# Merged first-layer matmuls in a Strassen-style MLP: products in a group of three and one of four per pair, preparation at earlier places

## The chip, the cores and the metric

The kernel runs on one core of a Trainium2 chip, in one launch. The metric is device time in microseconds (us) of an execution, as the median of three runs. The core has five engines that run side by side, each working through its own instructions in order: PE (TensorE, with the weight loads shown apart as PEld), DVE (VectorE), ACT (ScalarE), POOL (GpSimd) and SP (SyncE, which issues the DMAs here).

## What is computed

First an attention with random features (batch 8, 8 heads, 576 tokens, head size 64, 128 features), then a mixing of tokens through U and V, then an MLP over 8 * 576 = 4608 tokens with 512 inputs, 2048 hidden units and 512 outputs. The change touches the MLP:

```python
u = x + h.transpose(0, 2, 1)                    # x: attention output, h: token mixing
ch = np.maximum(u @ w_ch1, 0.0) @ w_ch2
return (u + ch).astype(np.float32)
```

Every float32 operand of a matmul is split into a high and a low part of a reduced format (fp32r), and a product is the sum of three passes: high weight with high data, high weight with low data, low weight with high data.

## The kernel before

**Stages.** Attention and token mixing run until about 380 us; then a whole pass of the MLP over the first 6 tiles of 128 tokens; from 443 to 1031 us seven **chunks** (c = 1 to 7) of 4 tiles (512 tokens); then a whole pass over the last 2 tiles (c = 8). The loop over chunks is at L1090. It is in the seven chunks that the change works, and in the last six of them that it changes the matmuls.

**A pair.** In a chunk the 16 blocks of hidden units are taken two at a time: eight **pairs** (p = 0 to 7). The first layer of a pair, a product of 2 x 2 blocks (inputs by hidden units by tokens), is made in Winograd's form with **seven products** (i = 0 to 6) in place of eight (`products`, L925). A product takes a data operand `self.ops[i]` (tiles `ux`, `uy`: sums of blocks of the transposed tokens, high and low, 2 halves of 128 inputs, 256 tokens) and a weight operand `w.ops[i]` (tile `wx`). It is six matmuls of 128x256: two halves by three passes. They accumulate in four PSUM banks X, Y, Z, W: products 0 and 3 in X, 1 and 4 in Y, 2 and 6 in Z, 5 in W. `after(i)` then takes a bank out: ACT copies (L938) and relus (L919), DVE sums (L774, in the helper `sums`) and the low part of the relu (L921). The results g of a pair are the data of the second layer.

**The order on PE.** The second layer of pair p is a generator of 24 matmuls of 128x512 (`second`, L987; 4 token tiles x 2 blocks x 3 passes, written to PSUM tiles `p_n` and `p_q`). `take(steps, 1)` places the next one of them into the stream. While the products of pair p+1 run, two or three second-layer matmuls of pair p stand between the six of each product and one more in `between(i)`. So a pair is 42 narrow and 24 wide matmuls.

**What else `between(i)` places (L1103).** Its steps stand on their engines in program order: fetching the weights of the next pair (`new.add()`: one DMA of 256 KB from `wx_dram` per product on SP, into a ring of 8 tiles, so that operand j of the next pair goes into the tile that operand j-1 of this pair leaves), stores of finished outputs (`stores`: a DVE sum L1008 and a DMA), and preparing the next chunk: `fetch` (L364: four DMAs on SP that bring 128 inputs of the next chunk's tokens into a tile `uraw`, of which there are two), `turn` (L858: a DVE transpose of a `uraw` tile into `uT`), `prepare` (L875: POOL sums of `uT` blocks) and `add` (L770 and L771: the split of an operand into high and low). Four `uraw` tiles are fetched per chunk, the third and fourth only behind the first and second turn, whose tiles they reuse. Turns stand in pairs 5 and 6 at i = 0 and 4, sums in pair 6, splits in pair 7.

Of the kernel before, what the change touches and what calls it, by code (L numbers as in the profile page):

```python
# [9 lines left out]
F32 = mybir.dt.float32  # L10
# [4 lines left out]
ALU = mybir.AluOpType  # L15
# [14 lines left out]
def performer_mlp_kernel(ctx: ExitStack, tc, q, k, v, omega, U, V, w1, w2, out):  # L30
# [27 lines left out]
    def f32(ap):  # L58
        return ap.bitcast(F32)
# [706 lines left out]
    keep = tc.keep_in_program_order  # L766

    def split(hl, x, rest=nc.gpsimd):

        keep(nc.scalar.copy(out=hl[:, 0], in_=x))  # L770
        keep(rest.tensor_tensor(out=hl[:, 1], in0=x, in1=f32(hl[:, 0]), op=SUBTRACT))  # L771

    def sums(out, a, b, op):
        keep(nc.vector.tensor_tensor(out=out, in0=a, in1=b, op=op))  # L774
# [64 lines left out]
    class Chunk:  # L839
# [37 lines left out]
        def prepare(self, part=(0, 1, 2)):  # L877

            for i in part:
                if i == 0:  # L880
                    self.sum(1, self.block(0, 1), self.block(0, 0), SUBTRACT)
                elif i == 1:
                    self.sum(2, self.block(1, 1), self.s[1], SUBTRACT)
                else:
# [12 lines left out]
        def whole1(self, w, between=lambda: None, every=lambda: None):  # L897
# [17 lines left out]
                between()  # L915
            return g

        def relu(self, g, ts, x, out=lambda: None):
            keep(nc.scalar.activation(out=g[:, 0, ts], in_=x, func=AF.Relu))  # L919
            out()  # L920
            keep(nc.vector.scalar_tensor_tensor(  # L921
                out=g[:, 1, ts], in0=x, scalar=0.0, in1=f32(g[:, 0, ts]), op0=ALU.max, op1=ALU.subtract
            ))

        def products(self, w, between, steps, out=lambda: None):  # L925

            bank = lambda n, b: ps.tile([P, HT], F32, name="p_s", tag=n, bufs=b)
# [6 lines left out]
            t1, t2 = slice(0, HT), slice(HT, TOK)  # L934

            def after(i):
                if i == 0:
                    keep(nc.scalar.copy(out=p1, in_=X))  # L938
                elif i == 1:
                    sums(u2, Y, p1, ADD)  # L940
                elif i == 3:
                    self.relu(g[0], t1, X)
                elif i == 4:
                    out()
                    sums(u3, Y, p1, ADD)
                    sums(c22, Z, u3, ADD)
                    self.relu(g[1], t2, c22, out)
                elif i == 5:
                    sums(c21, W, u3, ADD)
                    self.relu(g[1], t1, c21)  # L950
                elif i == 6:
                    sums(c12, Z, u2, ADD)
                    self.relu(g[0], t2, c12)

            for i, o in enumerate((X, Y, Z, X, Y, W, Z)):
                x, wt = self.ops[i], w.ops[i]
                for k in range(2):
                    for j, (l, r) in enumerate(passes((wt[:, 0, k], wt[:, 1, k]), (x[:, 0, k], x[:, 1, k]))):  # L960
                        tc.keep_in_program_order(nc.tensor.matmul(  # L961
                            o, l, r, start=(i in (0, 1, 2, 5) and k + j == 0), stop=(k == 1 and j == 2),
                            skip_group_check=True,
                        ))
                        if 3 * k + j in ((1, 3) if i % 2 else (0, 2, 3)):
                            take(steps, 1)
                after(i)
                between(i)
            return g

        def second(self, fs, gs, begin, end):
# [118 lines left out]
    for c in range(1, NCH - 1):  # L1090
        now, nxt = nxt, Chunk(c + 1)
        short = nxt.n < CT
        for p in range(NH):
            new = None
            if p + 1 < NH or not short:
                new = Weights(p + 1) if c == 1 and p + 1 < NH else Again((p + 1) % NH)
            if p < 2:
                nxt.fetch()
            if p == NH - 1:
                if not short:  # L1100
                    nxt.add()

            def between(i):  # L1103
                take(steps, 1)
                if p > 4 and i % 4 == 0 and nxt.turned < NC:
                    nxt.turn()
                    if nxt.turned < 3:
                        nxt.fetch()
                if p == 6 and not short and i in (2, 5, 6):
                    nxt.prepare([(2, 5, 6).index(i)])  # L1110
                if c == 1 and i < 2 and stores:
                    stores.pop(0)()
                if len(now.ops) < 7:
# [8 lines left out]
                for _ in range((0, 0, 0, 0, 0, 0, 2)[i] if c == 1 else 1):  # L1122
                    if stores:
                        stores.pop(0)()
                if p == NH - 1 and i < 6:
                    if not short:
                        nxt.add()
                    elif i in (0, 2):
                        nxt.short(nxt.uT[:, i : i + 2, :HT], nc.vector)
                    elif i in (1, 3):  # L1130
                        ws[i // 2] = Halves(i // 2)

            def out():
                if c == 1 and p == 0:
                    stores.pop(0)()

            g = now.products(pairs, between, steps, out)
# [47 lines left out]
```

## Time and profile before

| | us |
|---|---|
| runs before: median (lowest to highest of 3) | 1085.99 (1085.52 to 1086.03) |
| the profiled execution's own time | 1087.22 |
| its span in the trace | 1085.4 |
| PE busy, share of the span | 1074.5, 99% |
| DVE, ACT, POOL busy | 665.8, 502.3, 334.4 |
| from the first product of c = 1 to the last of c = 7 | 443.2 to 1030.8 |

The profile groups instructions by source line, engine and operation; "idle before" is time the engine stood still just ahead of them, with what ended it. A matmul's shown duration (280 ns for 128x256, some 393 ns for 128x512) is its whole way through the array, and matmuls overlap; what one costs is the distance from its start to the next one's start. The same holds in part on DVE.

### The profile page before, as it was taken

How to read it: one execution, taken by the hardware profiler on the slowest of the kernel's cores; microseconds unless marked ns; L12 is line 12 of the kernel's file. 1: busy time of each engine (PE TensorE's matmuls, PEld its weight loads, DVE VectorE, ACT ScalarE, POOL GpSimd, SP SyncE). 2: the span in 40 equal slices, each digit the busy share in tenths (PEclk: the TensorE clock that was granted, in tenths of full speed). 3: DMA queues.
4: the chain of work that ended last, by engine and by line, in shares of the span. 5: the costliest groups of instructions: out<-in, count | busy, mean ns of one | idle time of the engine just before them, and what ended most of it. 6: DMA issues, size and time to landing. Idle time of an engine off the chain costs nothing.

```text
span 1085.4 us, 20563 instructions
## 1 busy us (share of the span) xinstructions
PE 1074.5 (99%) x7119; PEld 974.3 (90%) x7119; DVE 665.8 (61%) x1460; ACT 502.3 (46%) x1417; POOL 334.4 (31%) x345
## 2 busy tenths in 40 slices
PE   9999999999999999999999999999999999999998
PEld 7899999999988888888888898988999888898987
DVE  4788998998977776655634734634643643643421
ACT  5799889998856664443321311311321321311232
POOL 3246547557445556565200100100100100100143
PEclk9999999999999999999999999999999999999999
DMA  8688887787224553565876876876885786785510
GB/s 138 129 149 146 169 177 150 172 169 130 79 86 141 146 149 94 201 216 195 254 212 173 251 218 156 257 232 156 234 256 166 221 254 163 216 253 158 181 59 20
DMA packets 344583, 187.93 MB, mean 173 GB/s; under 512 B 276128, under 2 KB 276128, under 8 KB 344480
## 3 DMA queue, kind: packets, MB, share of 16 engines
q1 hardware_dynamic: 342112, 186.32, 65.1%
q8 instruction: 57, 0.93, 0.4%
q10 hardware_dynamic: 2368, 0.30, 0.2%
q14 instruction: 46, 0.38, 0.1%
HBM read 152.99 MB, written 33.55 MB: 172 GB/s over the span
## 4 chain that ended last, share of the span: by engine, by line
PE 79%; DVE 4%; ACT 3%; POOL 2%; issue 2%; DMA 1%; SPq 0%; POOLq 0%; DVEq 0%; ACTq 0%
PE p_s L961 24%; PE p_n L987 17%; PE p_q L987 15%; PE p_p L910 6%; PE p_n L497 3%; PE p_kv L451 3%; PE p_p L539 2%; PE p_p L540 2%; PE p_p L541 2%; PE p_q L477 2%; PE py L334 2%; POOL mag L171 1%; DVE mag L149 1%; ACT e L554 1%; DMA kt<-in_k_dram 1%
## 5 line engine op out<-in xcount | busy, mean ns | idle before, releaser
L961 PE MATMUL p_s<-ux,wx 128*128 128x256 f32 x1728 | 363.8, 280 | 0.4 <-DVE far L774 0.3
L961 PEld LDWEIGHTS p_s<-ux,wx 128*128 128x128 f32 x1728 | 321.4, 188 | 31.6 <-DVE far L774 0.6
L987 PE MATMUL p_n<-w2h,g 128*128 128x512 f32 x576 | 219.1, 394 | 0.0
L987 PE MATMUL p_q<-w2h,g 128*128 128x512 f32 x512 | 195.4, 392 | 0.0
L554 ACT ACTIVATE e<-p_p,nm 128x128 f32<-128x128 f32 x576 | 166.3, 388 | 25.4 <-DVE nm L547 17.0
L961 PE MATMUL p_s<-uy,wx 128*128 128x256 f32 x624 | 132.6, 279 | 0.0
L420 POOL TENSOR_TENSOR xl<-xT,xh 128x384 fp32r<-128x384 f32 x95 | 94.5, 1014 | 116.7 <-ACT xh L416 90.8
L961 PEld LDWEIGHTS p_s<-uy,wx 128*128 128x128 f32 x624 | 117.0, 188 | 11.3 <-DMA wx<-wx_dram 0.3
L919 ACT ACTIVATE g<-far 128x256 fp32r<-128x256 f32 x112 | 46.8, 418 | 169.8 <-DVE far L774 169.8
L875 POOL TENSOR_TENSOR us<-uT 128x512 f32<-128x512 f32 x14 | 19.1, 1361 | 338.1 <-DVE uT L858 338.1
L987 PEld LDWEIGHTS p_n<-w2h,g 128*128 128x128 f32 x576 | 108.6, 188 | 9.3
L547 DVE TENSOR_REDUCE nm<-p_p 128x4 f32<-128x512 f32 x144 | 97.9, 680 | 25.5 <-PE p_p L541 16.9
L987 PE MATMUL p_n<-w2l,g 128*128 128x512 f32 x288 | 113.4, 394 | 0.0
L774 DVE TENSOR_TENSOR near<-p_s,near 128x256 f32<-128x256 f32 x168 | 70.3, 419 | 67.9 <-PE p_s L961 66.6
L771 POOL TENSOR_TENSOR wx<-w1f,wx 128x256 fp32r<-128x256 f32 x86 | 68.5, 811 | 135.1 <-ACT wx L770 133.5
L921 DVE SCALAR_TENSOR_TENSOR g<-p_s,g 128x256 fp32r<-128x256 f32 x56 | 23.7, 423 | 138.8 <-ACT g L919 138.7
L919 ACT ACTIVATE g<-p_s 128x256 fp32r<-128x256 f32 x56 | 21.5, 384 | 185.0 <-PE p_s L961 185.0
L987 PEld LDWEIGHTS p_q<-w2h,g 128*128 128x128 f32 x512 | 96.2, 188 | 9.9
L987 PE MATMUL p_q<-w2l,g 128*128 128x512 f32 x256 | 100.6, 393 | 0.0
L539 PE MATMUL p_p<-omh,xh 128*128 128x256 f32 x288 | 93.0, 323 | 1.7 <-ACT e L554 1.6
L910 PE MATMUL p_p<-ux,wx 128*128 128x512 f32 (+1 forms) x480 | 84.5, 326 | 0.2 <-DVE g L921 0.2
L921 DVE SCALAR_TENSOR_TENSOR g<-far,g 128x256 fp32r<-128x256 f32 x112 | 49.5, 442 | 53.9 <-ACT g L919 53.9
(133 smaller groups left out, 2055.8 us busy)
## 6 DMA issues: line engine op xcount, KB each, us to landing
wx<-wx_dram SPq DMA_DIRECT2D x336, 256.0 KB, 3.3
raw<-in_moe_w_ch_dram SPq DMA_DIRECT2D x32, 512.0 KB, 4.2
wx_dram<-wx SPq DMA_DIRECT2D x56, 256.0 KB, 2.0
u_dram<-x SPq DMA_DIRECT2D x36, 256.0 KB, 2.4
u<-u_dram SPq DMA_DIRECT2D x34, 256.0 KB, 4.6
out_dram<-u SPq DMA_DIRECT2D x34, 256.0 KB, 3.2
kt<-in_k_dram SPq DMA_DIRECT2D x120, 72.0 KB, 3.5
qt<-in_q_dram SPq DMA_DIRECT2D x120, 72.0 KB, 2.7
```

The costliest lines, as they stand in the source:

```text
L420: rest.tensor_tensor(out=self.xl[-1], in0=self.turned, in1=f32(self.xh[-1]), op=ALU.subtract)
L451: tc.keep_in_program_order(nc.tensor.matmul(o, e[:, h, :], w, start=(s == 0 and h == 0), stop=(s == NT - 1), skip_group_check=True))
L539: nc.tensor.matmul(o, part.xh[g][:, ts], oh, start=True, stop=False)
L547: nc.vector.tensor_reduce(out=self.nm[:, :n], in_=self.pp[:, :n], axis=AX.X, op=ALU.max, negate=True)
L554: nc.scalar.activation(out=self.e[:, j, :], in_=self.pp[:, j, :], func=AF.Exp, bias=self.nm[:, j : j + 1])
L771: keep(rest.tensor_tensor(out=hl[:, 1], in0=x, in1=f32(hl[:, 0]), op=SUBTRACT))
L774: keep(nc.vector.tensor_tensor(out=out, in0=a, in1=b, op=op))
L910: nc.tensor.matmul(ph, l, r, start=(cc + i == 0), stop=(cc == NC - 1 and i == 2))
L919: keep(nc.scalar.activation(out=g[:, 0, ts], in_=x, func=AF.Relu))
L921: keep(nc.vector.scalar_tensor_tensor(out=g[:, 1, ts], in0=x, scalar=0.0, in1=f32(g[:, 0, ts]), op0=ALU.max, op1=ALU.subtract))
L961: tc.keep_in_program_order(nc.tensor.matmul(o, l, r, start=(i in (0, 1, 2, 5) and k + j == 0), stop=(k == 1 and j == 2), skip_group_check= ...
L987: tc.keep_in_program_order(nc.tensor.matmul(po, l, r, start=(begin and n + i == 0), stop=(end and n == len(fs) - 1 and i == 2)))
```

## The change

For chunks 2 to 7, in all pairs but the last of a chunk (and in chunk 7 in that too), each product's passes are arranged otherwise. High and low parts of a data operand now lie side by side for each half, so one matmul of 128x512 with the high weight makes both "high with high" and "high with low" into the two halves of a full PSUM bank; a matmul of 128x256 with the low weight adds to the first half. A product is four matmuls in place of six. The two halves of a bank are added when it is taken out: more DVE sums, two more ACT copies, and the relu of product 3 reads the sum.

The matmuls are also regrouped. In pairs 0 to 5, products 0, 1, 2 form a group and 3, 4, 6, 5 another: all wide matmuls of the group, then all narrow ones, then twelve second-layer matmuls, then `after` and `between` for each of its products. In pair 6 (and 7 of chunk 7) there are four smaller groups. 43 pairs take the new form (five chunks of 7, one of 8); 13 keep the old one. The DVE part of a relu is put off behind the next product's sums (`pend`). For chunks from 2 on, turns move to pairs 2 and 3 at i = 2 and 6, sums to pairs 4 and 5 (the fourth sum gets a `uraw` tile of its own), the first split to pair 6, and stores to i = 1, 2, 5, 6.

```diff
-            split(self.slot(self.ops), x, nc.gpsimd if self.c == 1 and i in (3, 5) else nc.vector)
-            if i == 1:
+            op = self.slot(self.ops)
+            halve(op[:, :, 0], op[:, :, 1], x, nc.gpsimd if self.c == 1 and i in (3, 5) else nc.vector)
+            if i == 1 and 4 not in self.s:
...
+            bank = lambda n, b: ps.tile([P, 1 + bool(wide), HT], F32, name="p_s", tag=n, bufs=b)
...
+            def whole(to, o):
+                keep(nc.scalar.copy(out=to, in_=o[:, 0]))
+                if wide:
+                    sums(to, o[:, 1], to, ADD)
+
+            def add(to, o, x):
+                sums(to, o[:, 0], x, ADD)
+                if wide:
+                    sums(to, o[:, 1], to, ADD)
...
+                for group in wide:
+                    for i in group:
+                        for k in range(2):
+                            matmul(i, banks[i], w.ops[i][:, 0, k], self.ops[i][:, k], k == 0, False)
+                    for i in group:
+                        for k in range(2):
+                            matmul(i, banks[i][:, 0], w.ops[i][:, 1, k], self.ops[i][:, k, 0], False, k == 1)
+                    take(steps, (12 if len(wide) == 2 else 3 * len(group) + 1) - len(group))
+                    for i, j in zip(group, sorted(group)):
+                        after(i)
+                        between(j)
...
-                if p > 4 and i % 4 == 0 and nxt.turned < NC:
+                if p > (4 if c == 1 else 1) and i in ((0, 4) if c == 1 else (2, 6)) and nxt.turned < NC:
                     nxt.turn()
                     if nxt.turned < 3:
                         nxt.fetch()
-                if p == 6 and not short and i in (2, 5, 6):
+                if p == (6 if c == 1 else 4) and not short and i in (2, 5, 6):
                     nxt.prepare([(2, 5, 6).index(i)])
+                if p == 5 and c > 1 and not short and i == 2:
+                    nxt.prepare((3,))
+                if p == NH - 2 and not short and i == 3:
+                    nxt.add()
...
+            wide = () if c == 1 or p == NH - 1 and not short else ((0, 1, 2), (3, 4, 6, 5)) if p < 6 else ((0, 1), (2, 3), (4, 5), (6,))
```

**PE, within a pair of a chunk.** `p_s` rows are first-layer products, `p_n` and `p_q` rows the second layer. Before, from the middle of a pair:

```order
L961 MATMUL p_s<-ux,wx 128x256 x2
L987 MATMUL p_n<-w2h_5691,g 128x512
L961 MATMUL p_s<-ux,wx 128x256
L987 MATMUL p_n<-w2h_5707,g 128x512
L961 MATMUL p_s<-ux,wx 128x256 x2
L987 MATMUL p_n<-w2l_5708,g 128x512
```

And now, from the start of a pair:

```order
L994 MATMUL p_s<-ux,wx 128x512 x6
L994 MATMUL p_s<-ux,wx 128x256 x6
L1040 MATMUL p_n<-w2h_79,g 128x512
L1040 MATMUL p_n<-w2l_80,g 128x512
L1040 MATMUL p_n<-w2h_79,g 128x512
L1040 MATMUL p_n<-w2h_5707,g 128x512
```

The narrow matmuls stood singly or in twos between second-layer ones; now six wide and six narrow of one group stand together, and the second layer follows in one run.

**DVE, second half of a pair with a turn in it.** `near` and `far` hold the sums taken from the banks. Before:

```order
L858 STREAM_TRANSPOSE uT<-uraw 128x512
L774 TENSOR_TENSOR near<-p_s,near 128x256
L921 SCALAR_TENSOR_TENSOR g<-p_s,g 128x256
L774 TENSOR_TENSOR near<-p_s,near 128x256
L774 TENSOR_TENSOR far<-p_s,near 128x256
L921 SCALAR_TENSOR_TENSOR g<-far,g 128x256
L858 STREAM_TRANSPOSE uT<-uraw 128x512
```

Now, from the sums of product 3 to the end of the pair:

```order
L776 TENSOR_TENSOR near<-p_s,near 128x256 x3
L929 SCALAR_TENSOR_TENSOR g<-near,g 128x256
L776 TENSOR_TENSOR far<-near,far 128x256
L776 TENSOR_TENSOR far<-p_s,near 128x256
L776 TENSOR_TENSOR far<-p_s,far 128x256
L929 SCALAR_TENSOR_TENSOR g<-far,g 128x256
L776 TENSOR_TENSOR near<-p_s,near 128x256 x2
L929 SCALAR_TENSOR_TENSOR g<-far,g 128x256
L860 STREAM_TRANSPOSE uT<-uraw 128x512
L929 SCALAR_TENSOR_TENSOR g<-near,g 128x256
```

The second turn of a chunk stood behind the relu of product 4; now it stands behind the eight sums and the first three relu parts of the group 3, 4, 6, 5, as the last DVE step but one of pair 2.

**SP, the DMAs issued in the pair with two fetches.** The numbers behind `wx_dram` are pair weights: the digit is the operand. Before, in pair 5 (weights for pair 6):

```order
L364 DMA uraw<-u_dram_72 32x16x32 x4
L826 DMA wx<-wx_dram_0_5527 128x512
L826 DMA wx<-wx_dram_1_5528 128x512
L826 DMA wx<-wx_dram_2_5529 128x512
L826 DMA wx<-wx_dram_3_5530 128x512
L364 DMA uraw<-u_dram_72 32x16x32 x4
L826 DMA wx<-wx_dram_4_5531 128x512
L826 DMA wx<-wx_dram_5_5532 128x512
```

Now, in pair 2 (weights for pair 3):

```order
L364 DMA uraw<-u_dram_72 32x16x32 x4
L828 DMA wx<-wx_dram_2_5508 128x512
L828 DMA wx<-wx_dram_3_5509 128x512
L828 DMA wx<-wx_dram_4_5510 128x512
L828 DMA wx<-wx_dram_5_5511 128x512
L364 DMA uraw<-u_dram_72 32x16x32 x4
L828 DMA wx<-wx_dram_6_5512 128x512
```

The second fetch stood ahead of operand 4 of the next pair; now it stands ahead of operand 6.

More of the change, by code (lines that the diff above doesn't have):

```diff
@@ L768, in split, with halve @@
     def split(hl, x, rest=nc.gpsimd):
-        keep(nc.scalar.copy(out=hl[:, 0], in_=x))
-        keep(rest.tensor_tensor(out=hl[:, 1], in0=x, in1=f32(hl[:, 0]), op=SUBTRACT))
+        halve(hl[:, 0], hl[:, 1], x, rest)
+    def halve(h, l, x, rest):
+        keep(nc.scalar.copy(out=h, in_=x))
+        keep(rest.tensor_tensor(out=l, in0=x, in1=f32(h), op=SUBTRACT))
     def sums(out, a, b, op):
@@ L883, in prepare @@
                     self.sum(2, self.block(1, 1), self.s[1], SUBTRACT)
+                elif i == 3:
+                    out = late["rp"].tile([P, 2, HT], F32, name="uraw", bufs=2)
+                    self.sum(4, self.block(1, 0), self.s[2], SUBTRACT, out)
                 else:
@@ L916, in whole1, with relu, rest, products @@
             return g
-        def relu(self, g, ts, x, out=lambda: None):
+        def relu(self, g, ts, x, out=lambda: None, pend=None):
             keep(nc.scalar.activation(out=g[:, 0, ts], in_=x, func=AF.Relu))
             out()
[L921 to L927, printed above, removed]
+            def rest():
+                keep(nc.vector.scalar_tensor_tensor(
+                    out=g[:, 1, ts], in0=x, scalar=0.0, in1=f32(g[:, 0, ts]), op0=ALU.max, op1=ALU.subtract
+                ))
+            if pend is None:
+                rest()
+            else:
+                pend.append(rest)
+        def products(self, w, between, steps, out=lambda: None, wide=(), pend=None):
+            bank = lambda n, b: ps.tile([P, 1 + bool(wide), HT], F32, name="p_s", tag=n, bufs=b)
             X, Y, Z, W = bank("p_p", 2), bank("p_p", 2), bank("p_m", 1), bank("p_kv", 1)
@@ L939, in after @@
                 elif i == 1:
-                    sums(u2, Y, p1, ADD)
+                    add(u2, Y, p1)
+                elif i == 2:
+                    if wide:
+                        whole(c22, Z)
                 elif i == 3:
-                    self.relu(g[0], t1, X)
+                    if wide:
+                        whole(c21, X)
+                    self.relu(g[0], t1, c21 if wide else X[:, 0], pend=pend)
                 elif i == 4:
                     out()
-                    sums(u3, Y, p1, ADD)
@@ L946, in after @@
-                    sums(c22, Z, u3, ADD)
-                    self.relu(g[1], t2, c22, out)
+                    add(u3, Y, p1)
+                    flush()
+                    if wide:
+                        sums(c22, u3, c22, ADD)
+                    else:
+                        add(c22, Z, u3)
+                    self.relu(g[1], t2, c22, out, pend)
                 elif i == 5:
-                    sums(c21, W, u3, ADD)
-                    self.relu(g[1], t1, c21)
+                    add(c21, W, u3)
@@ L951, in after @@
+                    flush()
+                    self.relu(g[1], t1, c21, pend=pend)
                 elif i == 6:
[L952 to L968, printed above, removed]
+                    add(c12, Z, u2)
@@ new lines, in after, with matmul @@
+                    flush()
+                    self.relu(g[0], t2, c12, pend=pend)
+            def matmul(i, to, l, r, first, last):
+                tc.keep_in_program_order(nc.tensor.matmul(
+                    to, l, r, start=(i in (0, 1, 2, 5) and first), stop=last, skip_group_check=True
+                ))
+            banks = (X, Y, Z, X, Y, W, Z)
+            if wide:
+                for group in wide:
[9 more added lines that the diff above has]
+                        between(j)
+            else:
+                for i, o in enumerate(banks):
+                    x, wt = self.ops[i], w.ops[i]
+                    for k in range(2):
+                        for j, (l, r) in enumerate(passes((wt[:, 0, k], wt[:, 1, k]), (x[:, k, 0], x[:, k, 1]))):
+                            matmul(i, o[:, 0], l, r, k + j == 0, k == 1 and j == 2)
+                            if 3 * k + j in ((1, 3) if i % 2 else (0, 2, 3)):
+                                take(steps, 1)
+                    after(i)
+                    between(i)
@@ L969, in products @@
+            flush()
             return g
@@ L1121, in between @@
                             new.add()
-                for _ in range((0, 0, 0, 0, 0, 0, 2)[i] if c == 1 else 1):
+                for _ in range((0, 0, 0, 0, 0, 0, 2)[i] if c == 1 else i in (1, 2, 5, 6)):
                     if stores:
@@ L1135, in out @@
                     stores.pop(0)()
-            g = now.products(pairs, between, steps, out)
+            wide = () if c == 1 or p == NH - 1 and not short else ((0, 1, 2), (3, 4, 6, 5)) if p < 6 else ((0, 1), (2, 3), (4, 5), (6,))
+            g = now.products(pairs, between, steps, out, wide, [] if c > 1 else None)
             take(steps)
```

8 lines of the change are left out of this document (4 added, 4 removed).

## The prediction

> **What bounds the kernel now.** I read the busy times of the page first, then the stretch of the chunks alone, then who waited for whom in it.
>
> ```profile
> PE 1074.5 (99%) x7119; PEld 974.3 (90%) x7119; DVE 665.8 (61%) x1460; ACT 502.3 (46%) x1417; POOL 334.4 (31%) x345
> 610.86:946.86 336.00, 336.00 (x2113) 302.10 (x2112) 162.82 (x349) 77.82 (x188) 21.26 (x16) 1.00 0.75 213
> PEld p_s L961 <- DVE far L774: 0.6, 1, 0.6
> PEld p_s L961 <- issue: 0.5, 2, 0.3
> PEld p_s L961 <- DMA wx<-wx_dram: 0.3, 1, 0.3
> ```
>
> The second row is chunks 3 to 6 by themselves (columns: length, then busy time and count of PE, PEld, DVE, ACT, POOL, granted clock, DMA share, GB/s). PE is busy for all of the 336.00 us at full clock: 32 pairs of 66 matmuls at 10.50 us each. The last three rows are all that the weight loads waited for in the whole stretch of the chunks, 1.4 us. So PE's own pace is the bound: DVE (48% there), ACT and the DMAs are waited for nowhere. Two things can then change the time: the pace of the matmuls, and a wait that was not there.
>
> **The pace.** What matmuls cost in runs of one width is seen in the whole pass over the first six tiles, the nearest place to the new order.
>
> ```profile
> 380.78 0.40 PE L987 MATMUL p_n<-w2h,g 128*128 128x512 f32 x1
> ...
> 384.66 0.40 PE L987 MATMUL p_kv<-w2h,g 128*128 128x512 f32 x1
> 384.90 4.34 PE L910 MATMUL p_p<-ux,wx 128*128 128x512 f32 x24
> 389.07 0.40 PE L987 MATMUL p_n<-w2h,g 128*128 128x512 f32 x1
> ```
>
> From 380.78 to 384.90 run 18 matmuls of 128x512: 4.12 / 18 = 0.229 us from start to start. The row of 24 holds twelve of 128x512 and then twelve of 128x256 (it merges both); it takes 4.17, so the narrow ones take (4.17 - 12 x 0.229) / 12 = 0.119. A pair of the new form has 14 + 24 = 38 wide and 14 narrow matmuls: 38 x 0.229 + 14 x 0.119 = 10.36, against 10.50. That is 0.14 less, and 43 pairs give **6.1 us**. Two narrow ones at 0.119 are 0.238, so the merging itself saves little, 0.009 each; the rest is that narrow and wide no longer alternate. A wide product into a full PSUM bank isn't in the trace. Its bounds are 0.220 (256 more columns cost 0.229 - 0.119 = 0.110; twice that, with nothing per matmul) and 0.238 (no gain over two narrow ones); I take 0.229, its neighbour in shape. With 14 such in a pair these bounds move the pair by 0.13 either way, and the term runs from 0.6 to 11.5.
>
> The Trainium skill ("TensorE: Matmul & The Clock Gate", section "Back-to-back issue gap") gives N/2.4 + 2.5 ns for back-to-back matmuls at full clock, which is 0.216 and 0.109. By it a pair would save 28 x 0.109 - 14 x 0.216 = 0.04, and the term would be 1.6 in place of 6.1. The rows above are 6 to 9% slower than that, and they decide here.
>
> **What is added on DVE and ACT.** Distances between their starts, in an old pair with a turn:
>
> ```profile
> 765.53 0.42 DVE L774 TENSOR_TENSOR near<-p_s,near 128x256 f32<-128x256 f32 x1 [0.73 <-PE p_s L961]
> 765.99 0.42 DVE L774 TENSOR_TENSOR far<-p_s,near 128x256 f32<-128x256 f32 x1
> 766.45 0.42 ACT L919 ACTIVATE g<-far 128x256 fp32r<-128x256 f32 x1 [2.10 <-DVE far L774]
> 766.90 0.43 DVE L921 SCALAR_TENSOR_TENSOR g<-far,g 128x256 fp32r<-128x256 f32 x1 [0.49 <-ACT g L919]
> 767.25 0.70 DVE L858 STREAM_TRANSPOSE uT<-uraw 128x512 f32<-128x512 f32 x1
> 767.88 0.39 DVE L774 TENSOR_TENSOR near<-p_s,near 128x256 f32<-128x256 f32 x1
> ...
> 801.03 0.40 PE L961 MATMUL p_s<-ux,wx 128*128 128x256 f32 x2
> 801.47 0.37 ACT L938 COPY near<-p_s 128x256 f32<-128x256 f32 x1 [0.54 <-PE p_s L961]
> ```
>
> A DVE step that needs the one before it starts 0.46 behind it (765.53, 765.99); one that doesn't, 0.35 (766.90, 767.25). A relu starts 0.46 behind its sum, its DVE part 0.45 behind the relu, the step after a turn 0.63 behind it. An ACT copy (0.37) starts 0.04 after a product's matmuls end. A new pair has 12 sums and 4 relu parts in place of 5 and 4: 7 x 0.35 to 0.46, some 3 us more on an engine that had 5.4 us of 10.5 free. The cover is PE; what it costs is found by walking a pair, its start at 0.
>
> PE: 6 wide and 6 narrow to 2.09, twelve second-layer matmuls to 4.83, 8 wide to 6.66, 8 narrow to 7.61, twelve to 10.36. Product 3's last matmul starts at 6.78 and ends 0.28 later, at 7.06. DVE in the second group: ACT copy 7.10 to 7.47, the sum of product 3 at 7.50; then u3 at 7.85 and 8.31, relu part 8.66, c22 9.01, c12 9.36 and 9.82, relu part 10.17, c21 10.52 and 10.98, relu part 11.33, the last relu part at 11.9, done at 12.3. The next pair's second layer asks for that last part with its sixth matmul: 10.36 + 2.09 + 5 x 0.229 = 13.6, its weights 0.2 sooner. It is there 1.1 early. Banks are free long before their next group (Z is read until 10.2 and wanted at 11.27). So plain pairs wait for nothing: cost 0, and 0.35 us per step if the 1.1 us of cover were used up. A turn in between (0.63) or two stores (0.60 each, L1008) leave 0.1 to 0.7 of it. The earlier POOL sums, the earlier split and the fourth sum's tile cost nothing for the same reason: they stand where DVE idles from 4 to 7.5 in each pair, and a stall there would first have to outlast that.
>
> **The wait that is added.** The second turn of a chunk now comes at the end of that DVE chain in pair 2, and the fetch of the fourth `uraw` tile needs the tile that it frees. SP works in order: behind the four fetches stands operand 6 of pair 3, and behind that all loads for pair 4.
>
> ```profile
> 756.75 0.70 DVE L858 STREAM_TRANSPOSE uT<-uraw 128x512 f32<-128x512 f32 x1
> 757.48 1.91 SPq L364 DMA_DIRECT2D uraw<-u_dram  x4
> 757.60 1.29 POOL L875 TENSOR_TENSOR us<-uT 128x512 f32<-128x512 f32 x1 [67.72 <-DVE uT L858]
> 758.25 0.92 DVE L921 SCALAR_TENSOR_TENSOR g<-near,g 128x256 fp32r<-128x256 f32 x1 [0.49 <-ACT g L919]
> 759.49 4.73 SPq L826 DMA_DIRECT2D wx<-wx_dram  x8
> ...
> wx<-wx_dram SPq DMA_DIRECT2D x1, 256.0 KB, 2.7
> ...
> wx<-wx_dram SPq DMA_DIRECT2D x1, 256.0 KB, 3.4
> ...
> wx<-wx_dram SPq DMA_DIRECT2D x1, 256.0 KB, 4.4
> ```
>
> The old kernel shows the same chain: turn to 757.45, fetch issued 0.03 later, the next weights 2.01 behind the fetch. The last three rows are issue to landing of single `wx` loads that stand right behind such a fetch (issued at 667.5, 583.4, 591.3): shortest, middle and longest of eight that I looked up; their mean is 3.4. There it cost nothing: operand 4 landed at 759.49 + 3.0 = 762.5, and four of seven products of a pair of 10.5 stand ahead of its use, 6 us from that pair's start at 757.86, which is 763.9.
>
> In the new pair 2 the turn starts 0.35 behind the relu part at 11.33, at 11.68, and ends at 12.38. Fetch at 12.41, operand 6 issued at 14.42, landed at 17.1 to 18.8, by the mean at 17.85. PE wants it for product 6, third of the second group of pair 3: 10.36 + 4.83 + 4 x 0.229 = 16.10. PE stands still for **1.75 us** (1.0 to 2.7), and products 6 and 5 and all second-layer matmuls behind them with it. This comes once in each of chunks 2 to 6; in chunk 7, whose next chunk is half as wide, I count half, 0.9. Together 5 x 1.75 + 0.9 = 9.6 us (5.5 to 15). The first fetch of pair 2 delays operand 2 in the same way, but from a turn that ends at 4.5: it lands at about 10, and is wanted at 11.27.
>
> **Sum.** -6.1 + 9.6 = +3.5 us. The profiled execution (1087.22, of which 1085.4 is span) would become 1090.7; against the median of 1085.99 I predict 1089.5. A run of this kernel can tell about 0.2%, 2.2 us, from no change.
>
> **Rivals.**
> - *Short waits.* The loads land as the quickest ones do (2.7): 1.0 per chunk, 5.5 in all, and the sum is -0.6: 1085.4. For it: in the new order no other weight load is under way when the fetch starts. Against: one of the eight rows is that short. With half of the pace term gone too it stays within 2 us of before. Chance 0.22.
> - *No wait: faster.* Operand 6 is there in time if SP issues it before 16.10 - 3.4 = 12.7, so if the turn ends by 10.6, 1.8 before the walk has it: were DVE's steps to overlap more than the rows show, or another hold-up of PE in pair 2 or 3 to hide the landing. Then only the pace is left: 1085.99 - 6.1 = 1079.9. For it: nothing else in the walk makes PE wait. Against: the chain's distances are measured, and SP's order is fixed. Chance 0.18.
> - *DVE late as well.* Row 758.25 took 0.92 in place of 0.42 beside a POOL sum. In pair 0 two stores stand in the chain and leave 0.1 to 0.3 us; a delay of 0.5 there would stop PE by some 0.3 in each of six chunks, 2 us more: 1091.5. Chance 0.05.
> - *The pace is set by columns alone.* Then wide matmuls take twice a narrow one, the pace term falls to 1.6 or less, and the waits stay: 1085.99 - 1.6 + 9.6 = 1094. Against: 0.229 and 0.238 above. Chance 0.03. The skill's gap, cited above, would give this.
>
> **How the numbers follow.** The forecast, a wait of 1.4 to 2.7 per chunk, gets 0.52. Forecast, DVE late and columns alone are slower: 0.60. Short waits are the same: 0.22. No wait is faster: 0.18. The range goes from 1083.5 (quick landings with the whole pace term) to 1094.5 (the slowest landings): it holds the widest pace term with the middle wait (1084.1), and leaves out the rival without a wait and little above.
>
> **What will show it.** In the new trace: pairs 0, 1, 4 and 5 of a chunk at 10.36 us (pace right), 10.5 (wrong); DVE with some 16 steps per plain pair and PE without a gap there; in pair 3 of chunks 2 to 6 one gap of PE of 1 to 2.7 us ahead of a `p_s` row, put down to the DMA of `wx`, with the turn of pair 2 ending some 12.4 into that pair. No such gap, and a time near 1080, would make the prediction wrong; so would gaps put down to DVE.

## The result and the profile after

| | before | after |
|---|---|---|
| median of the runs, us (lowest to highest of 5) | 1085.99 (1084.86 to 1087.33) | 1099.86 (1097.42 to 1101.96) |
| ratio, 95% interval | | 1.0125 (1.0112 to 1.0138) |
| span of the profiled execution | 1085.4 | 1098.1 |
| start of the first product of c = 1 | 443.24 | 443.28 |
| from there to the start of the last product matmul of c = 7 | 587.56 | 599.46 |

The kernel became slower by 13.9 us. The direction was forecast; the size was not, since the range ended at 1094.5. Of the 12.7 us that the span grew, 11.9 lie in the seven chunks. Below this stretch is called the **stage**: it is the cleaner measure, because the code ahead of it is the same in every kernel here. In the new form three second-layer matmuls of the last pair come behind the stage's end (21 in place of 24 stand ahead of it); these three, some 0.7 us, are nearly all of the 0.8 between 11.9 and 12.7. So a stage of a new-form kernel looks 0.7 us shorter than it is beside before's.

The busy times of the page of after:

```profile
PE 1071.0 (98%) x6517; PEld 946.0 (86%) x6517; DVE 757.5 (69%) x1761; ACT 536.3 (49%) x1503; POOL 332.6 (30%) x345
```

PE has 602 matmuls fewer, and only 3.5 us less work in a span that is 12.7 longer: it waits now. Three pairs by windows of after, cut at the start of the first product of each, show where (a plain pair 5 of chunk 3, pair 3 of chunk 4, pair 0 of chunk 5):

```profile
core 0: us, PE busy (x) PEld busy (x) DVE busy (x) ACT busy (x) POOL busy (x), PEclk, DMA share, GB/s
667.86:678.19 10.33, 10.33 (x53) 8.81 (x52) 6.05 (x17) 2.79 (x8) 0.00 (x0) 1.00 0.54 181
731.65:743.74 12.09, 10.58 (x53) 8.72 (x52) 7.16 (x19) 2.78 (x8) 1.29 (x1) 1.00 0.72 209
785.25:797.22 11.97, 10.59 (x55) 8.73 (x53) 7.55 (x20) 3.46 (x9) 0.00 (x0) 1.00 0.92 278
```

The plain pair has no idle PE: 10.33 us where the old one had 10.50. The other two are 1.76 and 1.64 longer, at full clock. The waits of PE and of its weight loads in the stage of after (sum, count, longest):

```profile
PEld p_s L994 <- issue: 21.4, 14, 1.9
...
PE p_s L994 <- issue: 8.4, 6, 1.5
PE p_s L994 <- DMA wx<-wx_dram: 7.6, 7, 1.5
...
PEld p_s L994 <- DVE far L776: 1.1, 2, 0.7
...
PE p_s L994 <- DVE far L776: 0.4, 1, 0.4
```

Six of the seven waits for `wx` are the forecast ones, in pair 3 of chunks 2 to 7; the seventh, 0.4 us, is in pair 2 of chunk 7. The six put down to "issue", 8.4 us, were not forecast, and the view names no cause for them. A pair grows by more than the idle time of the view: that begins only when the shown 0.39 of the last matmul is over, where the next would have started after 0.23, and the first matmul behind a stop is followed after 0.31. Together this is some 0.24 more per stop.

**The forecast gap.** Timeline of after, end of pair 2 and first half of pair 3 of chunk 4 (the pairs start at 721.32 and 731.65):

```profile
732.83 0.71 DVE L860 STREAM_TRANSPOSE uT<-uraw 128x512 f32<-128x512 f32 x1
...
733.56 1.91 SPq L364 DMA_DIRECT2D uraw<-u_dram  x4
...
735.58 2.33 SPq L828 DMA_DIRECT2D wx<-wx_dram  x5
...
736.47 1.07 PE L994 MATMUL p_s<-uy,wx 128*128 128x512 f32 x4
...
739.05 1.16 PE L994 MATMUL p_s<-ux,wx 128*128 128x512 f32 x4 [1.51 <-DMA wx<-wx_dram]
```

This is the chain that the prediction walked. The turn ends at 733.54, the fetch is issued at 733.56, and operand 6 of pair 3 only at 735.58; it landed at 738.91, and PE, which had been ready at 737.54, stood still for 1.51 us.

**The gap that was not forecast.** Timeline of after at the border from pair 7 of chunk 4, which keeps the old form, to pair 0 of chunk 5, which has the new one and starts at 785.25 (the first row merges the last narrow matmuls of the one and the first wide ones of the other):

```profile
785.02 1.31 PE L994 MATMUL p_s<-ux,wx 128*128 128x256 f32 x6
...
785.62 0.42 ACT L925 ACTIVATE g<-near 128x256 fp32r<-128x256 f32 x1 [1.09 <-DVE near L776]
785.95 0.60 ACT L772 CAST ux<-uT 128x512 fp32r<-128x512 f32 x1
...
786.58 0.69 DVE L773 TENSOR_TENSOR ux<-uT,ux 128x512 fp32r<-128x512 f32 x1 [0.66 <-ACT ux L772]
787.19 0.42 DVE L776 TENSOR_TENSOR far<-p_s,near 128x256 f32<-128x256 f32 x1
...
787.68 0.76 PEld L994 LDWEIGHTS p_s<-ux,wx 128*128 128x128 f32 x4 [1.77 <-issue]
787.71 0.82 PE L994 MATMUL p_s<-ux,wx 128*128 128x512 f32 x3 [1.38 <-issue]
```

Product 6 is the last of an old-form pair and lies in bank Z. The row at 787.19 is the DVE sum that takes it out. It stands behind the split of an operand (786.58), that behind ACT's cast (785.95), and the cast behind the relu of product 5 (785.62). It ends at 787.61, 2.36 us into the new pair, and 0.10 later PE goes on. The new pair wants Z for its product 2 after four wide matmuls, two for each of products 0 and 1: 4 x 0.229 = 0.92 us in. The old kernel had the same chain at the same border (timeline of before, pair 0 starting at 778.86):

```profile
780.54 0.42 DVE L774 TENSOR_TENSOR far<-p_s,near 128x256 f32<-128x256 f32 x1
```

There Z came free 2.10 us in, about as late, but two whole products with their second-layer matmuls, some 3 us, stood ahead of its use. The reading was that regrouping moved the use forward, not that the sum became late.

The lengths of all pairs, start to start, add up: 36 pairs at 10.33 and 7 in four groups at 10.36 would save 0.17 x 36 + 0.14 x 7 = 7.1 us; pair 0 of chunks 2 to 7 is 9.9 longer than that pace, pair 3 of the same chunks 8.7 (single lengths from 11.51 to 12.09), pair 2 of chunk 7 0.7; the old-form pairs of chunk 1 lose 0.6, and the last pair wins 0.7 beyond its pace, by the three matmuls behind the end of the stage. Together +12.1, against 11.9 measured.

### The profile page after: what moved, and what is told of

It reads as the page before. It is cut to its first block, busy times and chain, and to the rows that moved or that the text cites. A ratio compares the mean times of both kernels' runs of the same rounds, so it can differ in the third digit from the quotient of the medians.

```text
span 1098.1 us, 19981 instructions
## 1 busy us (share of the span) xinstructions
PE 1071.0 (98%) x6517; PEld 946.0 (86%) x6517; DVE 757.5 (69%) x1761; ACT 536.3 (49%) x1503; POOL 332.6 (30%) x345
## 4 chain that ended last, share of the span: by engine, by line
PE 71%; DVE 9%; ACT 6%; DMA 5%; issue 4%; POOL 3%; SPq 2%; POOLq 0%; DVEq 0%; ACTq 0%
PE p_s L994 20%; PE p_n L1040 15%; PE p_q L1040 11%; PE p_p L916 5%; PE p_kv L451 4%; PE p_n L497 3%; DMA wx<-wx_dram 3%; PE p_p L539 3%; PE p_p L540 2%; PE p_p L541 2%; PE p_q L477 2%; PE py L334 2%; ACT e L554 1%; DVE g L929 1%; POOL mag L171 1%
## 5 line engine op out<-in xcount | busy, mean ns | idle before, releaser
L994 PE MATMUL p_s<-ux,wx 128*128 128x256 f32 (+1 forms) x1282 | 264.2, 319 | 11.2 <-issue 5.5
L994 PEld LDWEIGHTS p_s<-ux,wx 128*128 128x128 f32 x1282 | 220.8, 188 | 45.1 <-issue 14.4
L776 DVE TENSOR_TENSOR near<-p_s,near 128x256 f32<-128x256 f32 x383 | 158.3, 421 | 141.4 <-ACT near L954 127.2
L1040 PE MATMUL p_n<-w2h,g 128*128 128x512 f32 x576 | 198.6, 392 | 0.0
L1040 PE MATMUL p_q<-w2h,g 128*128 128x512 f32 x512 | 177.2, 391 | 0.0
L954 ACT COPY near<-p_s 128x256 f32<-128x256 f32 x99 | 36.8, 371 | 185.8 <-PE p_s L994 185.8
L994 PE MATMUL p_s<-uy,wx 128*128 128x512 f32 (+1 forms) x468 | 105.6, 318 | 5.4 <-issue 2.9
L994 PEld LDWEIGHTS p_s<-uy,wx 128*128 128x128 f32 x468 | 82.3, 189 | 17.2 <-issue 7.0
L916 PEld LDWEIGHTS p_p<-ux,wx 128*128 128x128 f32 x480 | 73.8, 190 | 9.4 <-DVE g L929 0.6
L540 PE MATMUL p_p<-oml,xh 128*128 128x256 f32 x288 | 81.8, 284 | 0.0
```

Of the source, the lines that this page charges most:

```text
L540: nc.tensor.matmul(o, part.xh[g][:, ts], ol, start=False, stop=False)
L916: nc.tensor.matmul(ph, l, r, start=(cc + i == 0), stop=(cc == NC - 1 and i == 2))
L994: tc.keep_in_program_order(nc.tensor.matmul(to, l, r, start=(i in (0, 1, 2, 5) and first), stop=last, skip_group_check=True))
L1040: tc.keep_in_program_order(nc.tensor.matmul(po, l, r, start=(begin and n + i == 0), stop=(end and n == len(fs) - 1 and i == 2)))
```

## The experiments

Theory at this point: two gaps of equal size, the weights behind the fetch (pair 3) and the bank Z (pair 0), and a pace gain of 7 us under them. Rivals: the cast, or the `uraw` DMA that is under way at the border, holds pair 0; the pace comes from the regrouping and not from the merging; the earlier preparation is what costs.

| run | median, us | ratio to before (95%) | stage, us |
|---|---|---|---|
| after | 1099.86 | 1.0125 (1.0112 to 1.0138) | 599.46 |
| e1: weights ahead of the fetch | 1090.58 | 1.0043 (1.0029 to 1.0057) | 591.49 |
| e2: sum of Z ahead of the split | 1093.84 | 1.0084 (1.0063 to 1.0106) | 592.30 |
| e3: both | 1084.29 | 0.9979 (0.9970 to 0.9989) | 584.79 |
| e4: old matmuls, new places | 1089.88 | 1.0034 (1.0021 to 1.0048) | 589.62 |
| e5: e1, pair 0 in four groups | 1084.36 | 0.9978 (0.9968 to 0.9987) | 584.30 |
| e6: e3, grouped but unmerged | 1092.02 | 1.0046 (1.0029 to 1.0062) | 592.01 |
| e7: e5, two edits more | 1084.24 | 0.9975 (0.9964 to 0.9987) | 583.75 |
| e8: e5, preparation at old places | 1089.03 | 1.0024 (1.0012 to 1.0036) | 588.78 |
| e9: e7, pair 0 in two groups | 1080.59 | 0.9948 (0.9934 to 0.9961) | 582.17 |

Before had a stage of 587.56 (all but e4 leave out the three second-layer matmuls, 0.7 us, that it holds). Each ratio of e1 to e9 is to executions of the kernel before on the same chip.

### e1: the weights ahead of the fetch

```diff
-                if p > (4 if c == 1 else 1) and i in ((0, 4) if c == 1 else (2, 6)) and nxt.turned < NC:
+                if c == 1 and p > 4 and i in (0, 4) and nxt.turned < NC:
                     nxt.turn()
...
                     new.add()
...
+                if c > 1 and p > 1 and i in (2, 6) and nxt.turned < NC:
+                    nxt.turn()
+                    if nxt.turned < 3:
+                        nxt.fetch()
```

> The changed kernel, but for chunks from 2 on the next pair's weight load is issued ahead of a turn and its fetches, not behind them; nothing else moves. Theory (order on SP: operand 6 of pair 3 is late because four fetches that wait for the turn stand ahead of it): the gap of 1.1 to 1.7 us in pair 3 of chunks 2 to 6 goes, and so does that of chunk 7: about 8.5 us less than the changed kernel, 1091, with the gap of 1.54 us at the start of pair 0 left as it is. Rival (the fetches take the DMA engines from the weights, in whatever order they are issued): the gap stays above 1 us or moves to operands 0 to 2 of the next pair, and the time stays within 2 us of 1099.9.

Measured: 1090.58, as the theory had it, the stage 8.0 us shorter. The fetch costs SP what it did, but stands behind the weights; and in the waits of the stage `wx` nearly disappears while "issue" stays as it was:

```profile
731.51 1.91 SPq L364 DMA_DIRECT2D uraw<-u_dram  x4
...
PE p_s L994 <- issue: 8.4, 6, 1.5
PE p_s L994 <- DMA wx<-wx_dram: 0.6, 1, 0.6
```

Pair 3 of chunk 4 is 10.33 long, pair 0 still 11.97. So the gap in pair 3 was the order on SP, and the gap in pair 0 has nothing to do with it. Some 1.3 us came back in pair 2 of chunks 2 and 5 (10.77 and 11.17), the latter put down to `wx`; why the loads land late there was not looked into.

### e2: the sum of Z ahead of the split

Operand 6 is split at i = 6, behind product 6's sum, and no longer at i = 5 ahead of it.

```diff
-                if p == NH - 1 and i < 6:
+                if p == NH - 1 and i != (6 if short else 5):
```

> The changed kernel, but in pair 7 of a chunk the sixth split of the next chunk's data (operand 6) stands behind the sums of product 6, not ahead of them. Theory (product 2 of pair 0 waits for bank Z, whose last reader, the DVE sum of product 6, is queued behind a DVE step that waits for ACT's cast): the gap of 1.54 us at the start of pair 0 goes in chunks 2 to 7, about 9.3 us less than the changed kernel, 1090.5, and the gaps in pair 3 stay. Rival (PE waits for data: the cast that the trace names as the one that ended the wait): the cast now comes later, so the gap stays or grows, and the time is 1100 or more.

Measured: 1093.84, the stage 7.2 shorter. The waits turn round:

```profile
PE p_s L994 <- DMA wx<-wx_dram: 7.2, 6, 1.7
PE p_s L994 <- issue: 0.7, 1, 0.7
```

Pair 0 went from some 11.96 to 10.60 to 10.66 (11.31 in chunk 2), and the six waits for "issue" to one. So they were the bank: the cast now comes later and the gap is gone, and the `uraw` fetch at the border starts 0.88 us into pair 0 as it did before the edit (781.08 here, 786.13 in after). The stage gained 7.2 and not the 9.9 of the gap because pair 0 keeps 0.3 in each of chunks 3 to 7 and 1.0 in chunk 2; pair 1 of chunk 4 is also 0.36 longer.

### e3: both

> Both edits together. Theory (two separate waits, and under them the pace of 10.33 us per pair): the gains add up, 1099.9 - 8.5 - 9.3 = 1082, that is 0.996 of the kernel before; no gap over 0.3 us left in chunks 3 to 6. Rival (a third wait lies close behind these, such as DVE's last relu part or the next weights): at least 3 us of it come back as gaps elsewhere, 1085 or more, no faster than before.

Measured: 1084.29, 0.2% below before, between the theory's 1082 and the rival's 1085. The stage is 14.7 shorter than after's; the two alone made 8.0 + 7.2 = 15.2, so the gaps are nearly independent. Timeline and waits of e3 at the same border (pair 0 starts at 778.08):

```profile
778.67 0.42 DVE L776 TENSOR_TENSOR far<-p_s,near 128x256 f32<-128x256 f32 x1
...
779.16 1.00 PEld L994 LDWEIGHTS p_s<-ux,wx 128*128 128x128 f32 x6 [0.43 <-ACT g L925]
779.45 0.61 ACT L772 CAST ux<-uT 128x512 fp32r<-128x512 f32 x1
...
PE p_s L994 <- issue: 0.7, 1, 0.7
PE p_s L994 <- DMA wx<-wx_dram: 0.6, 3, 0.2
```

Z is free at 779.09, 1.01 us in, and the weights behind it load at 779.16, before the cast has begun: the cast isn't what PE waited for. What is left is 0.3 in pair 0 of chunks 3 to 7 (10.62 to 10.66), 0.98 in chunk 2's, and 0.3 to 0.5 in pair 1 of chunks 4 to 6 and pair 2 of chunks 3 and 5, three of these five put down to `wx`. Chunk 2's pair 0 (start 527.17) is held by the same bank. It follows chunk 1, which does not put off the relu's DVE part, and the sum of Z stands behind that part:

```profile
528.10 0.43 DVE L929 SCALAR_TENSOR_TENSOR g<-near,g 128x256 fp32r<-128x256 f32 x1 [0.48 <-ACT g L925]
...
528.45 0.42 DVE L776 TENSOR_TENSOR far<-p_s,near 128x256 f32<-128x256 f32 x1
...
528.96 0.70 PE L994 MATMUL p_s<-uy,wx 128*128 128x512 f32 x2 [0.71 <-issue]
```

So the loss follows the time at which Z is free: 2.36 us in costs 1.63 (after), 1.70 costs 0.98, 1.01 costs 0.3, each some 0.2 more than the delay beyond 0.92.

### e4: the old matmuls, with the new places of the preparation

```diff
-            wide = () if c == 1 or p == NH - 1 and not short else ((0, 1, 2), (3, 4, 6, 5)) if p < 6 else ((0, 1), (2, 3), (4, 5), (6,))
+            wide = ()
```

> The changed kernel with the old matmuls in all pairs (six narrow ones per product, second layer between them); the earlier preparation, the put-off relu parts and the layout of the data stay. Theory (the moved steps cost only where the new grouping asks sooner for operand 6 and for bank Z): pairs back at 10.50 us and no gap in pair 3 or pair 0 over 0.3 us; the time of the kernel before within 2 us, 1086. Rival (the earlier preparation itself makes PE wait): some 8 us above the kernel before, 1094, with the gaps in pair 3 still there.

Measured: 1089.88, which neither theory has. No gap in pair 3: with alternating matmuls product 6 comes last in the pair, so the late weights hide, as they did before. But pair 0 of chunks 3 to 7 is 10.95 long. Timeline of e4:

```profile
614.13 0.69 DVE L773 TENSOR_TENSOR ux<-uT,ux 128x512 fp32r<-128x512 f32 x1 [0.66 <-ACT ux L772]
...
614.74 0.42 DVE L776 TENSOR_TENSOR far<-p_s,near 128x256 f32<-128x256 f32 x1
...
615.08 0.41 DVE L929 SCALAR_TENSOR_TENSOR g<-near,g 128x256 fp32r<-128x256 f32 x1
...
615.54 0.50 PE L1040 MATMUL p_n<-w2h,g 128*128 128x512 f32 x1 [0.18 <-DVE g L929]
```

A second-layer matmul waits for a relu part that the change puts off behind the next product's sum; here that sum stands behind the same split. That this costs the 0.47 of pair 0 is read from the timeline and was not tried by itself; for it speaks that pair 0 of chunk 2, behind chunk 1 where no relu part is put off, is 10.50 long. 0.47 x 5 and 0.6 in chunk 1, less 0.02 in each of the other pairs of chunks 3 to 6 and less 0.4 that the kernel before loses in pair 6 of chunks 2 and 6, make the 2.1 us of the stage, within 0.1; another 1.6 us of the profiled execution lie ahead of the stage (it starts at 444.81), in code that is the same (see the last section).

### e5: e1, with pair 0 in four groups

```diff
-            ... ((0, 1, 2), (3, 4, 6, 5)) if p < 6 else ((0, 1), (2, 3), (4, 5), (6,))
+            ... ((0, 1, 2), (3, 4, 6, 5)) if 0 < p < 6 else ((0, 1), (2, 3), (4, 5), (6,))
```

> The run with weights issued first, and in pair 0 of a chunk the products in four groups of two, two, two and one, so that PE asks for bank Z (product 2) some 3.0 us into the pair, not 0.92; the split of operand 6 stands where the change has it. Theory (product 2 waits for the DVE sum that empties bank Z, which ends 2.4 us into pair 0): the gap at the start of pair 0 goes without any step of DVE or ACT being moved, pair 0 at 10.4 to 10.5 us in place of 12.0: 9 us less than the 1090.6 of the run with weights first, 1081.5. Rival (PE waits there for data or for the engines being behind in general): pair 0 keeps 1 us or more of its gap, 1087 or more.

Measured: 1084.36 for some 1081.5 expected. With groups of two, seven second-layer matmuls stand ahead of product 2, and the sum of Z no longer holds it. Pair 0 of chunk 5 starts at 776.31:

```profile
778.25 0.42 DVE L776 TENSOR_TENSOR far<-p_s,near 128x256 f32<-128x256 f32 x1
...
778.58 0.42 DVE L929 SCALAR_TENSOR_TENSOR g<-near,g 128x256 fp32r<-128x256 f32 x1
...
779.05 0.73 PE L1040 MATMUL p_n<-w2h,g 128*128 128x512 f32 x2
```

Z is free at 778.67, 2.36 us in as in after, and pair 0 is 10.68 to 10.73 long in chunks 3 to 7. That it gains no more than e3 was missed: a second-layer matmul (779.05) now waits for the relu part at 778.58, which costs 0.35 in pair 0, and product 6 is last in four groups, so pair 1 finds Z late by 0.2 in its turn (10.64). The gap moved on by a pair and shrank.

### e6: grouped, but not merged

e3 with each wide high-weight matmul cut into its two narrow ones:

```diff
                         for k in range(2):
-                            matmul(i, banks[i], w.ops[i][:, 0, k], self.ops[i][:, k], k == 0, False)
+                            for a in range(2):
+                                matmul(i, banks[i][:, a], w.ops[i][:, 0, k], self.ops[i][:, k, a], k + a == 0, False)
```

> The run with both edits (weights first, bank first), but each wide first-layer matmul cut into two of 128x256, one for each half of the bank; groups, sums and everything else as there. It tells merging from regrouping. Theory (spacing of 0.118 for narrow and 0.228 for wide wherever they stand): a pair goes from 10.33 to 10.33 + 14 x (0.236 - 0.228) = 10.45 us, 43 pairs 5 us more than with both edits, 1089; so two thirds of the pace term are the merging. Rival (as the prediction had put it, that most of it comes from narrow and wide no longer alternating): a pair stays within 0.04 of 10.33, and the time within 2 us of 1084.3.

Measured: 1092.02 for some 1089 expected. A plain pair by windows of e6:

```profile
665.60:676.12 10.52, 10.52 (x68) 9.54 (x67) 6.06 (x17) 2.79 (x8) 0.00 (x0) 1.00 0.49 172
```

PE works without a gap, takes 10.52, and the old kernel took 10.50: setting narrow matmuls together gains nothing. The step from 10.52 to 10.33 is all merging, 0.19 a pair or 0.014 for each of 14. A merged matmul also needs one weight load in place of two; which of the two savings it is was not separated.

### e7: two edits more on e5

The first split goes back to the start of pair 7 for chunk 1, the fetches of pairs 0 and 1 go into pair 1 behind its weights.

```diff
-            if p < 2:
+            if c == 1 and p < 2:
                 nxt.fetch()
+            if c == 1 and p == NH - 1:
+                nxt.add()
...
-                if p == NH - 2 and not short and i == 3:
+                if c > 1 and p == NH - 2 and not short and i == 3:
                     nxt.add()
...
+                if c > 1 and p == 1 and i in (2, 6):
+                    nxt.fetch()
```

> The run with four groups in pair 0, and two more edits: in chunk 1 the first split of the next chunk goes back to the start of pair 7, and in chunks from 2 on the first two fetches stand in pair 1 behind its weight loads, not at the starts of pairs 0 and 1 beside the loads of the residual. Theory (all that is left between the new kernel and its pace are the 0.6 us of chunk 1 and the 0.3 to 0.5 us gaps where weights of pairs 1 and 2 land late): chunks 2 to 7 at 10.33 to 10.5 us in every pair, 1080, that is 0.9945 of the kernel before. Rival (the small gaps come from DVE or the turns of pair 2 now find their data late): no better than the run with four groups.

Measured: 1084.24 for some 1080 expected, not to be told from e5. Chunk 1 is 0.4 us shorter and the stage 0.55 (583.75 for 584.30). The moved fetches gained nothing: e5's pairs 1 and 2 were already alike in all chunks (10.64 and 10.33), without late landings. What the theory left out are the 0.36 and 0.31 of pairs 0 and 1 above.

### e8: e5 with the preparation at its old places

Turns in pairs 5 and 6, sums in pair 6, first split at the start of pair 7, as before the change.

```diff
+            if p == NH - 1 and not short:
+                nxt.add()
...
-                if p > (4 if c == 1 else 1) and i in ((0, 4) if c == 1 else (2, 6)) and nxt.turned < NC:
+                if p > 4 and i in (0, 4) and nxt.turned < NC:
...
-                if p == (6 if c == 1 else 4) and not short and i in (2, 5, 6):
+                if p == 6 and not short and i in (2, 5, 6):
                     nxt.prepare([(2, 5, 6).index(i)])
-                if p == 5 and c > 1 and not short and i == 2:
-                    nxt.prepare((3,))
-                if p == NH - 2 and not short and i == 3:
-                    nxt.add()
```

> The run with four groups in pair 0, but with the preparation of the next chunk at the places of the kernel before (turns in pairs 5 and 6 at i = 0 and 4, POOL sums in pair 6, fourth sum and all splits in pair 7, turns ahead of the weights). It asks whether preparing sooner helps the merged matmuls at all. Theory (POOL's sums then stand against DVE steps with two inputs in SBUF, and the first split waits for them): gaps of 0.5 to 2 us per chunk in pairs 6 and 7, put down to DVE, 1085 to 1093. Rival (it is not needed): within 2 us of the run with four groups.

Measured: 1089.03, within what the theory had, the stage 4.5 longer than e5's. Pair 6 of chunks 2 to 6 is 11.06 long (10.36 in e5), pair 7 10.64 (10.48): 4.3 us in all. Pair 1 of chunk 6, with a late `wx`, loses 0.6 more, and chunk 1 wins 0.5. Timeline of e8, pair 6 of chunk 3:

```profile
674.65 0.70 DVE L860 STREAM_TRANSPOSE uT<-uraw 128x512 f32<-128x512 f32 x1
...
675.50 1.29 POOL L877 TENSOR_TENSOR us<-uT 128x512 f32<-128x512 f32 x1 [67.60 <-DVE uT L860]
...
676.04 1.03 DVE L929 SCALAR_TENSOR_TENSOR g<-far,g 128x256 fp32r<-128x256 f32 x1
...
677.90 0.42 ACT L925 ACTIVATE g<-near 128x256 fp32r<-128x256 f32 x1 [1.33 <-DVE near L776]
...
678.37 0.50 PE L1040 MATMUL p_n<-w2h,g 128*128 128x512 f32 x1 [0.42 <-ACT g L925]
```

A turn and a relu part that took 1.03 beside a POOL sum, in place of 0.42, stand in the DVE chain that a new-form pair fills; the last relu comes late for the second layer. So the earlier preparation does help the merged form, by some 4 us; the second fetch in front of operand 6 was its price, and not one that it had to pay.

### e9: two groups in pair 0 as well

e7 with e2's order of the split, and two groups in pair 0, but for chunk 2, where e3 had still lost 0.98:

```diff
-            ... if 0 < p < 6 else ((0, 1), (2, 3), (4, 5), (6,))
+            ... if p < 6 and (c, p) != (2, 0) else ((0, 1), (2, 3), (4, 5), (6,))
...
-                if p == NH - 1 and i < 6:
+                if p == NH - 1 and i != (6 if c == 1 or short else 5):
```

> As the run called e7, but pair 0 of chunks 3 to 7 is back in the groups of three and four, with the split of operand 6 behind the sums of product 6 in pair 7 (as in the run with both edits); chunk 2 keeps four groups in pair 0 and its old split order. Theory (four groups in pair 0 cost 0.36 us there, by the data of its second layer, and 0.31 in pair 1, because product 6 then comes last and empties bank Z late; the bank-first order costs 0.3 in pair 0 and nothing in pair 1): pair 0 at 10.62 and pair 1 at 10.33 in chunks 3 to 7, 2 us less between the first and the last product than the 583.75 of e7, 581.9; in time 1082, 0.9955 of the kernel before. Rival (weights of pairs 1 and 2 land late again, as in the run with both edits, since more of the loads come while pair 0 runs faster): pairs 1 and 2 show gaps of 0.3 to 0.5 us, and the stretch is as long as in e7.

Measured: 1080.59 (1080.15 to 1082.26), 0.5% faster than before (0.9948, 0.9934 to 0.9961) and 1.8% than after; the stage is 582.17 for 581.9 expected. The page, two windows (pair 4, and pair 0 of chunk 5) and the one wait of a product that PE itself still shows in the stage:

```profile
PE 1068.1 (99%) x6517; PEld 944.8 (88%) x6517; DVE 754.4 (70%) x1761; ACT 536.2 (50%) x1503; POOL 332.4 (31%) x345
...
733.76:744.09 10.33, 10.33 (x53) 8.80 (x52) 6.56 (x18) 2.79 (x8) 3.79 (x3) 1.00 0.59 201
775.27:785.88 10.61, 10.58 (x54) 8.73 (x53) 7.36 (x20) 3.45 (x9) 0.00 (x0) 1.00 0.88 285
...
PE p_s L994 <- DVE far L776: 0.3, 1, 0.3
```

Pairs 1 to 5 of chunk 4 are all 10.33; pair 0 keeps 0.28. With the order on SP and on DVE mended, the merged form brings two thirds of what its pace promises: the stage is 5.4 us shorter than before's, 4.7 without the three matmuls that it leaves out, where the pace is worth 7.1. The small gaps that are left (pair 0 of every chunk, pair 1 of chunk 2, pair 2 of chunk 5) are 2.5.

## Why the prediction was right in its direction and wrong in its size

- **The pace: right, and a little small.** Forecast 10.36 for a plain pair and 6.1 us, measured 10.33 (10.36 in four groups) and 7.1. The sentence on its source was wrong: "the merging itself saves little, 0.009 each; the rest is that narrow and wide no longer alternate". By its own numbers 14 x 0.009 is 0.126 of the 0.14, so hardly any rest was left, and e6 shows that regrouping gains nothing. The old pair could have told it: 10.50 less 24 x 0.229 leaves 0.119 for each of its 42 narrow matmuls, the pace that the prediction took for a long run.
- **Columns alone, and the Trainium skill's gap** ("TensorE: Matmul & The Clock Gate", section "Back-to-back issue gap"), which that section calls the gap of an isolated matmul. By it a pair would win 14 x 2.5 ns = 0.035, some 1.5 us in all (the prediction has 0.04 and 1.6). The traces disagree with it: a pair won 0.17, and the spacings here are 0.229 and 0.119 where it has 0.216 and 0.109.
- **Plain pairs wait for nothing: right.** 17 DVE steps, and no gap of PE in the rows above. In pair 2 of chunk 4 the last relu part, which there stands behind a turn, was done 12.5 us into the pair (the walk has 12.3 without a turn), and the next pair asked for it a good 1 us later, as it says. "The earlier split", put at nothing, was not free in chunk 1: pair 6 there is 11.20 long for 10.48 before, and with the split moved back (e7) 10.50. Pair 7 gets part of it back, and 0.4 to 0.6 us remain.
- **The added wait: right in its place and mechanism, and nearly in its size.** In pair 3 of chunk 4 the turn ends 12.22 into pair 2 (forecast 12.38), operand 6 is issued at 14.26 (14.42), landed at 17.59 (17.85), wanted at 16.22 (16.10): PE idle for 1.51 us and the pair 1.76 longer, where 1.75 stood. Over chunks 2 to 6 pair 3 lost 1.5 on average, and in chunk 7 1.4, where half was counted: 8.7 in all against 9.6. e1 took the gap away in every chunk, and 8.0 us off the stage. The late operand in pair 2 of chunk 7 (0.7) was not forecast.
- **The step that failed is "Banks are free long before their next group (Z is read until 10.2 and wanted at 11.27)".** This holds for a new-form pair behind a new-form pair, which is the only border that was walked. Pair 0 follows pair 7, which keeps the old form: there product 6 is last, its sum stands behind the split and the cast, and Z is free 2.36 us into the next pair, where the sentence has it free 0.2 ahead of that pair's start. This cost some 1.6 us in each of six chunks, 9.9 in all; e2 and e3 moved that one split and took 7.4 of it away, and e5, which left the split and asked for Z later, took 7.5 away there, of which 1.9 came back in pair 1. The sum of +3.5 lacked this term: 3.5 + 9.9 = 13.4, against 12.7 of span and 13.9 of the medians. (The lower end of the range, 1083.5, does not follow from its terms: quick landings with the whole pace term give 1085.4, as the first rival has it.)
- **The rivals.** "DVE late as well" put its stop in the right pair for another reason (a slowed relu part, 0.3 each) and at a fifth of the price. "No wait", 1079.9, is near what the kernel does with both gaps closed, e9's 1080.59, but that it is so near is luck: e9 has a pace worth 7.1 and not 6.1, and 2.5 of small gaps are left in it.

## What to carry to other kernels

When a change moves reads of a buffer to the front of a block, walk each border between blocks, above all where the form changes, and ask of each buffer who empties it and what is queued ahead of that instruction on its engine; one steady-state walk misses what happens once per outer loop. On an in-order DMA queue, put the loads that the next block needs ahead of a transfer that waits for a late result. The gap that the view put down to "issue" had a cause: look in the timeline for the last step that ended just before such a gap ends, and move that step alone.

## What the runs showed of the hardware

- The four DMAs of one fetch (64 KB each) hold SP's queue for 1.9 to 2.0 us (733.56 and 786.13 in after, 731.51 in e1), where one weight load of 256 KB takes 0.32 (783.82 in after).
- A matmul of 128x256 with its own weights takes no less time in a long run of its kind than between wide ones: 0.120 worked out for e6's plain pair, (10.52 - 24 x 0.229) / 42, and 0.119 for the alternating pair above.
- Behind a stop, the second matmul of 128x512 starts 0.31 us after the first, not 0.23 (after: 787.71 and 739.05).
- A DVE step of 0.42 us took 1.03 beside a POOL sum (e8, 676.04), more than the 0.92 of the prediction's row.
- The part ahead of the stage, the same code in all kernels, ended between 441.5 and 445.1 us in the profiled executions, 3.6 us apart and more than e3 differs from before. The granted clock of that part goes with it. It was 0.96 from 20 to 50 us and again from 50 to 100 in e4 and e8 (444.8 and 445.1); 0.96 to 0.98 in the first stretch and 0.98 to 0.99 in the second in before, after, e1 and e6 (443.2 to 443.6); and 1.00 in both in e2, e5, e7 and e9 (441.5 to 442.2). e3, at 1.00 and 443.15, does not fit, and why is open. From 445 to 1020 us it is 1.00 in every one, so the stage's own length is the better witness for differences of 0.2%.
